# Copying one set of mask rows on VectorE in slot 22 instead of with a DMA

## The chip, the cores and the metric

The kernel runs on one NeuronCore of one Trainium2 chip. The metric is the device time of one execution in microseconds (us), taken as the median of several runs. Five engines run their own instruction streams: TensorE (PE, with its weight loads shown as PEld), VectorE (DVE), ScalarE (ACT), GpSimd (POOL) and SyncE (SP), which here issues DMAs and does nothing else.

## What is computed

Block-sparse attention is followed by a gated feed-forward layer with spatial mixing:

```python
# q, k, v: (batch 4, heads 8, seq 768, dim 64); blocks of 32, so 24 blocks
scores = np.matmul(q, k.transpose(0, 1, 3, 2)) / np.sqrt(64)
mask = near_diagonal | first_or_last_block | sampled_blocks     # per (query block, key block)
attn = softmax(np.where(mask, scores, -1e9))
x = concat_heads(attn @ v)                                       # (4, 768, 512)
h = np.maximum(x @ w_in, 0)                                      # (4, 768, 1024)
u, vv = h[..., :512], h[..., 512:]
vn = (vv - mean(vv)) / np.sqrt(var(vv) + 1e-6)
out = (u * (w_spatial @ vn + b_spatial)) @ w_out
```

## The kernel before, in words

**The mask as matmul rows.** One SBUF tile, `kq`, holds for each of the 8 heads the transposed keys (768 columns, `K_`) and the transposed queries (768 columns, in three thirds of 256 that `qcols(t)` names). Its partitions 0 to 63 are the head dimension. Its partitions 64 to 87 (`MR`) are 24 "block rows": on the key side a one-hot code of the key's block, on the query side the mask value of that query's block against each of the 24 key blocks. A matmul over all 88 partitions so gives score plus mask at once. The block rows are the same for every head and every batch, so they are made once for head 0 and then copied to the other heads. Who copies which piece, and when, differs from piece to piece:

- head 1 gets its rows by VectorE copies (`rows(H1, ...)`) ahead of the loop;
- heads 2 and 3, second query third, by a DMA that SP issues (`rows_dma(1, 4)`);
- heads 2 to 7, third query third, by another DMA that SP issues (`rows_dma(2, H)`); it stands in SP's order behind the last load of `w_in` and in front of the load of `b_col`;
- all other pieces by VectorE copies (`rows`, line 248) in slots that the list `ROWS` names.

**Slots.** The main loop `for s in range(...)` goes through slots. In each slot PE makes one score tile (`qk_unit`, line 446, in slots 0 to 35, where the first batch is done by thirds of the queries; `qk_full`, line 459, after that), ACT takes its exponential, PE makes earlier attention products (`av_unit`, line 492; `av_full`, line 510), then the functions registered with `when(slot, ...)` run, then some steps of the feed-forward layer (`run_queue`, line 584, with the counts of `STEPS`), then the functions in `late`. The order in which this Python code runs is the order of each engine's instructions; nothing is reordered later. The third query third of head 2 is first read by `qk_unit` in slot 27 (unit 9, that is heads 2 and 3).

**What stands in slots 13 to 32 for batch 1 (pairs 4 and 5) and the spatial weights.** SP's order after `rows_dma(2, H)` is: `b_col` (line 364); the loads of pair 4, k, q and v (line 109, slot 13); six loads `ws_f` of the spatial weights (line 550, slots 16 to 18); the DMA transpose `tr_dma` of pair 4 (line 417, slot 20); the loads of pair 5 (slot 22); transposes of the spatial weights (line 560). POOL's order is: the last casts of `w_in` (line 234) and of pair 0's remaining query columns; the casts of pair 4 (line 137, slot 18); `ws_cast` 0, 1 and 2 (line 556, slots 19, 21, 23); the reciprocal deviation `std`, `rstd` of the first two feed-forward rows (lines 623 and 625, slot 23); `ws_cast` 3 (slot 25); the casts of pair 5 (slot 26). VectorE normalises these rows with `rstd` (`vn<-vn,mv,rstd`, line 186), copies the transposed keys and queries of pair 4 into `kq` (`split`, line 218, slots 31 and 32), and empties PSUM banks of the attention product (`xt<-ps_av`, line 218), which PE needs back.

In slot 21 VectorE copies the last queries of pair 0 (`tr_rest(0)`, two copies `kq<-ps_av`). In slot 22 the next VectorE instruction is the ReLU of the feed-forward row v1 (`vn<-ps_moe`, line 186).

Of the kernel before, what the change touches and what calls it, by code (L numbers as in the profile page):

```python
# [26 lines left out]
def kernel(  # L27
# [16 lines left out]
    nc = tc.nc  # L44

    B, H, S, D = q.shape
    BLK = 32
    NB = S // BLK
# [16 lines left out]
    TW = TC * 128  # L65
# [17 lines left out]
    kq = const.tile([KR, H, 2 * S], BF16, name="kq")  # L83
    NVV = 6
    vv = [const.tile([128, 2, NCH, VS], BF16, name=f"vv{s}") for s in range(NVV)]
    MR = slice(D, KR)
    K_, Q_ = slice(0, S), slice(S, 2 * S)

    def qcols(t0, n=1):
        return slice(S + t0 * TW, S + (t0 + n) * TW)  # L90
# [27 lines left out]
    def cast(p, nm, eng, hs=BOTH, cs=ALLC):  # L118
        if nm == "v":
            dst = vv[p % NVV][:, hs, cs, 0:D]  # L120
        else:
            if p not in nat:
                nat[p] = work.tile([128, 2 * NCH, 2, D], BF16, tag="nat", bufs=4, name="nat")
            c0 = 0 if nm == "k" else NCH
            dst = nat[p][:, c0 + cs.start:c0 + cs.stop].rearrange("p c h d -> p h c d")[:, hs]
        src = st[nm, p].rearrange("p h (c d) -> p h c d", d=D)[:, hs, cs]
        if p == 0 and nm != "v":
            dst = nat0_view()[:, hs, (c0 + cs.start) * D:(c0 + cs.stop) * D]
            if cs is not C45:
                dst = dst[:, 0].rearrange("p (i t d) -> p t i d", t=2, d=D)  # L130
                src = src[:, 0].rearrange("p (t i) d -> p t i d", t=2)
            else:
                dst = dst.rearrange("p h (c d) -> p h c d", d=D)
        if eng is nc.scalar:
            nc.scalar.activation(out=dst, in_=src, func=AF.Copy)
        else:
            eng.tensor_copy(out=dst, in_=src)  # L137
# [92 lines left out]
    def w_in_load(u, g):  # L230
        w_load((u, g), moe_w_in[g * 128:(g + 1) * 128, 0 if u else DH:DH if u else DFF])
# [11 lines left out]
    def rows(hs, cs, eng=nc.vector):  # L243
        src = kq[MR, 0:1, cs].to_broadcast([NB, hs.stop - hs.start, cs.stop - cs.start])
        if eng is nc.scalar:
            nc.scalar.activation(out=kq[MR, hs, cs], in_=src, func=AF.Copy)
        else:
            eng.tensor_copy(out=kq[MR, hs, cs], in_=src)  # L248

    def rows_dma(t, h1):  # L250
        nc.sync.dma_start(out=kq[MR, 2:h1, qcols(t)],
                          in_=kq[MR, 0:1, qcols(t)].to_broadcast([NB, h1 - 2, TW]))

    cast(0, "k", nc.scalar, H0, C03)
    cast(0, "q", PL, H0, C03)
    rows(H1, K_)
# [72 lines left out]
    m1()  # L329
    m2()  # L330
    rows(H1, qcols(0, 3))
    rows_dma(1, 4)
    w_in_load(0, 1)
    load(2, "q", cs=C25)
    w_in_load(0, 2)
# [14 lines left out]
    cast(3, "v", PL)  # L350
    w_in_cast(0, 1, PL)
    w_in_load(1, 2)
    rows_dma(2, H)
    cast(2, "q", PL, cs=C25)
    w_in_cast(0, 2, PL)
    w_in_cast(0, 3, PL)
# [376 lines left out]
    def when(slot, *fns):  # L733
        at.setdefault(slot, []).extend(fns)

    def c(f, *a, **kw):
        return lambda: f(*a, **kw)

    ROWS = [(1, 2, 4, qcols(0)), (1, 2, 3, K_), (3, 3, 4, K_), (4, 4, 6, qcols(0)), (6, 4, 6, K_), (7, 6, 8, qcols(0)), (9, 6, 8, K_), (15, 4, 8, qcols(1))]
    when(0, second)  # L740
    when(1, third)
    when(2, lambda: filler(FILL3, psum.tile([128, 512], FP32, tag=moe_tag(), bufs=1, name="wps")))
# [3 lines left out]
    when(10, c(tr_first, 3))  # L746
    for sl, h0, h1, cs in ROWS:
        when(sl, c(rows, slice(h0, h1), cs))
# [146 lines left out]
```

## Time and profile before

| | |
|---|---|
| median of 3 runs | 211.81 us (211.39 to 212.13) |
| the profiled execution | 212.83 us |
| its span, first to last instruction | 209.9 us, so 2.9 us lie around it |
| granted TensorE clock, mean | 0.997 |
| busy: PE, PEld, DVE, ACT, POOL | 200.5, 127.1, 133.7, 167.7, 69.7 us |

Busy times are sums over the span. They do not say where the time is set: that is read from the chain of waits and from the idle gaps of PE, stage by stage. All durations below are of the one profiled execution.

### The profile page before, as it was taken

To read this page: it belongs to the slowest core of one execution; us is meant where nothing else is said; L and a number is where in the kernel's file an instruction comes from. 1 tells how busy PE (TensorE), PEld (TensorE's weight loads), DVE (VectorE), ACT (ScalarE), POOL (GpSimd) and SP (SyncE) were. 2 spreads that over 40 slices of the span, in tenths; PEclk is the share of its full clock that TensorE was granted. 3 is DMA by queue.
4 is the path that set the end of the run, shared out by engine and by line. 5 is a ranking of instruction groups with operands and counts; after the bars stand their busy time and mean duration, and the time that the engine had idled before them with its cause. 6 is when DMAs were issued, how large, how long until landed. Compare 5 with 4: busy or idle time off the path is not lost.

```text
span 209.9 us, 5241 instructions
## 1 busy us (share of the span) xinstructions
PE 200.5 (96%) x2107; PEld 127.1 (61%) x2141; DVE 133.7 (64%) x294; ACT 167.7 (80%) x222; POOL 69.7 (33%) x108
## 2 busy tenths in 40 slices
PE   7898999899999999999999999999999999999992
PEld 6597878666666666665565556665565556544441
DVE  7899675988864545484986464375884443476551
ACT  5898999899989989989998888979999787266021
POOL 6685759675564123033065050131020000012000
PEclk9999999999999999999999999999999999999998
DMA  5999899999999999999955597795101225520275
GB/s 146 343 363 324 279 352 253 272 232 249 275 350 241 257 185 285 242 293 336 209 194 112 131 246 167 202 269 159 37 3 35 52 53 118 196 78 0 50 191 211
DMA packets 64356, 41.93 MB, mean 200 GB/s; under 512 B 45196, under 2 KB 59084, under 8 KB 64332
## 3 DMA queue, kind: packets, MB, share of 16 engines
q1 hardware_dynamic: 63756, 41.01, 75.7%
q10 hardware_dynamic: 576, 0.59, 0.8%
q8 instruction: 16, 0.26, 0.6%
q14 instruction: 8, 0.07, 0.1%
HBM read 24.38 MB, written 6.29 MB: 146 GB/s over the span
## 4 chain that ended last, share of the span: by engine, by line
PE 78%; DVE 6%; DMA 5%; POOL 3%; SPq 2%; issue 2%; ACT 1%; ACTq 0%; DVEq 0%
PE ps_moe L584 29%; PE ps L459 22%; PE ps_av L510 12%; PE ps_t L584 8%; PE ps_sc L584 4%; DMA ws_f<-in_moe_w_spatial_dram 3%; POOL ws_b L556 2%; DVE kq L218 2%; DMA st_q<-in_q_dram 2%; DVE vn L186 2%; SPq L109 2%; PE ps_av L492 1%; PE ps L446 1%; DVE kq L248 1%; PE ps L293 1%
## 5 line engine op out<-in xcount | busy, mean ns | idle before, releaser
L463 ACT ACTIVATE a_all<-ps 128x768 bf16<-128x768 f32 x144 | 113.6, 812 | 14.5 <-PE ps L459 8.2
L459 PE MATMUL ps<-kq 88*128 88x384 bf16 x288 | 70.4, 325 | 0.4
L510 PEld LDWEIGHTS <-a_all 128*128 128x128 bf16 x864 | 45.2, 97 | 20.0
L510 PE MATMUL ps_av<-vv,a_all 128*128 128x65 bf16 x864 | 49.8, 193 | 0.0
L459 PEld LDWEIGHTS <-kq 88*128 88x128 bf16 x288 | 27.7, 98 | 29.6
L584 PE MATMUL ps_moe<-w_in_t,xt 128*128 128x512 bf16 x127 | 38.6, 378 | 0.5
L451 ACT ACTIVATE a_all<-ps 128x1024 bf16<-128x1024 f32 x36 | 34.2, 1026 | 3.0 <-PE ps L446 2.7
L584 PE MATMUL ps_moe<-vn,w_spt 128*128 128x512 bf16 x99 | 30.2, 378 | 0.4
L137 POOL CAST nat<-st_k 128x768 bf16<-128x768 f32 (+2 forms) x17 | 13.2, 781 | 39.6 <-DMA st_k<-in_k_dram 38.0
L446 PE MATMUL ps<-kq 88*128 88x256 bf16 (+1 forms) x140 | 21.6, 275 | 2.0 <-ACT a_all L451 0.9
L656 DVE SCALAR_TENSOR_TENSOR un<-ps_moe,b_col,un 128x512 bf16<-128x512 f32 x18 | 13.4, 746 | 13.6 <-PE ps_moe L584 11.3
L623 POOL TENSOR_SCALAR std<-mv 128x3 f32<-128x3 f32 (+1 forms) x9 | 2.2, 240 | 58.2 <-DVE mv L620 41.1
L474 DVE RECIPROCAL rc<-ps_av 128x6 f32<-128x6 f32 (+1 forms) x36 | 6.6, 183 | 21.5 <-PE ps_av L510 20.0
L584 PEld LDWEIGHTS <-xt 128*128 128x128 bf16 x192 | 15.5, 98 | 7.6 <-DVE xt L218 0.2
L584 PE MATMUL ps_moe<-w_out_t,gt 128*128 128x512 bf16 x66 | 19.7, 378 | 0.2
L475 DVE TENSOR_TENSOR xn<-ps_av,rc 128x384 bf16<-128x384 f32 (+1 forms) x36 | 18.5, 513 | 1.2
L137 POOL CAST nat<-st_q 128x768 bf16<-128x768 f32 (+2 forms) x21 | 14.8, 706 | 8.5 <-DMA st_q<-in_q_dram 8.2
L619 DVE BATCH_NORM_STATS2 stats<-vn 128x6 f32<-128x512 bf16 x24 | 16.4, 684 | 1.3 <-ACT vn L614 0.9
L137 POOL CAST vv<-st_v 128x768 bf16<-128x768 f32 x16 | 13.8, 863 | 9.4 <-DMA st_v<-in_v_dram 9.0
L186 DVE TENSOR_SCALAR vn<-vn,mv,rstd 128x512 bf16<-128x512 bf16 x24 | 14.0, 615 | 4.4 <-POOL rstd L625 4.4
L218 DVE COPY kq<-tt 64x1536 bf16<-64x1536 bf16 x24 | 14.8, 618 | 2.9 <-DMA tt<-nat 2.6
L446 PEld LDWEIGHTS <-kq 88*128 88x128 bf16 x140 | 12.5, 97 | 5.8 <-DVE kq L218 1.9
(81 smaller groups left out, 202.5 us busy)
## 6 DMA issues: line engine op xcount, KB each, us to landing
st_v<-in_v_dram SPq DMA_DIRECT2D x16, 384.0 KB, 6.1
st_k<-in_k_dram SPq DMA_DIRECT2D x15, 384.0 KB, 4.5
out_dram<-osb SPq DMA_DIRECT2D x22, 256.0 KB, 3.1
st_q<-in_q_dram SPq DMA_DIRECT2D x12, 384.0 KB, 5.6
ws_f<-in_moe_w_spatial_dram SPq DMA_DIRECT2D x6, 384.0 KB, 7.6
w_f<-in_moe_w_in_dram SPq DMA_DIRECT2D x8, 256.0 KB, 5.5
w_f<-in_moe_w_out_dram SPq DMA_DIRECT2D x4, 256.0 KB, 4.0
st_q<-in_q_dram SPq DMA_DIRECT2D x6, 128.0 KB, 5.8
```

Of the source, the lines that this page charges most:

```text
L137: eng.tensor_copy(out=dst, in_=src)
L186: nc.vector.tensor_scalar(out=out, in0=in0, scalar1=s1, scalar2=s2, op0=o0, **kw)
L218: nc.vector.tensor_copy(out=o, in_=i)
L446: nc.tensor.matmul(out=ps[:, at:at + n * TW], lhsT=kq[:, h, ci * 128:(ci + 1) * 128], rhs=kq[:, h, qcols(t0, n)], start=True, stop=True)
L451: nc.scalar.activation(out=out, in_=ps, func=AF.Exp, scale=0.125)
L459: nc.tensor.matmul(out=ps[:, hf * 512:hf * 512 + HALF], lhsT=kq[:, j % H, ci * 128:(ci + 1) * 128], rhs=kq[:, j % H, S + hf * HALF:S + (hf ...
L463: nc.scalar.activation(out=a_ref["h", j][:, ci, :].rearrange("p (b c) -> p b c", b=2), in_=ps.rearrange("p (b c) -> p b c", b=2)[:, :, 0:H ...
L475: nc.vector.tensor_tensor(out=out, in0=ps[:, :, 0:D], in1=rc[:, 0:n].to_broadcast([128, n, D]), op=ALU.mult)
L510: nc.tensor.matmul(out=av_ref[j][:, qc, 0:VA], lhsT=a_ref["h", j][:, ci, qc * 128:(qc + 1) * 128], rhs=vv[p % NVV][:, h, ci, 0:VA], start= ...
L584: nc.tensor.matmul(out=ref["ps"][:, 0:w], lhsT=lhs(i), rhs=rhs(i), start=(i == 0), stop=(i == n - 1))
L619: nc.vector.bn_stats(out=stats, in_=self.vn[:, tcc, :])
L656: nc.vector.scalar_tensor_tensor(out=self.un[:, tcc, :], in0=ps, scalar=b_col[:, tcc:tcc + 1], in1=self.un[:, tcc, :], op0=ALU.add, op1=AL ...
```

## The change

The DMA for heads 2 to 7 of the third query third goes out of SP's order. In its place the list `ROWS` gets one more entry, so VectorE makes the same copy (24 partitions, 6 heads of 256 columns) in slot 22. The helper `rows_dma` goes away; its other use is written out and stays what it was.

```diff
-    def rows_dma(t, h1):
-        nc.sync.dma_start(out=kq[MR, 2:h1, qcols(t)],
-                          in_=kq[MR, 0:1, qcols(t)].to_broadcast([NB, h1 - 2, TW]))
...
     rows(H1, qcols(0, 3))
-    rows_dma(1, 4)
+    nc.sync.dma_start(out=kq[MR, 2:4, qcols(1)],
+                      in_=kq[MR, 0:1, qcols(1)].to_broadcast([NB, 2, TW]))
...
     w_in_load(1, 2)
-    rows_dma(2, H)
     cast(2, "q", PL, cs=C25)
...
-    ROWS = [(1, 2, 4, qcols(0)), ... (9, 6, 8, K_), (15, 4, 8, qcols(1))]
+    ROWS = [(1, 2, 4, qcols(0)), ... (9, 6, 8, K_), (15, 4, 8, qcols(1)), (22, 2, 8, qcols(2))]
     when(0, second)
     when(1, third)
...
     for sl, h0, h1, cs in ROWS:
         when(sl, c(rows, slice(h0, h1), cs))
```

More of the change, by code (lines that the diff above doesn't have):

```diff
@@ L737, in c @@
         return lambda: f(*a, **kw)
-    ROWS = [(1, 2, 4, qcols(0)), (1, 2, 3, K_), (3, 3, 4, K_), (4, 4, 6, qcols(0)), (6, 4, 6, K_), (7, 6, 8, qcols(0)), (9, 6, 8, K_), (15, 4, 8, qcols(1))]
+    ROWS = [(1, 2, 4, qcols(0)), (1, 2, 3, K_), (3, 3, 4, K_), (4, 4, 6, qcols(0)), (6, 4, 6, K_), (7, 6, 8, qcols(0)), (9, 6, 8, K_), (15, 4, 8, qcols(1)), (22, 2, 8, qcols(2))]
     when(0, second)
```

## The prediction

> **What bounds the kernel now.** I read the busy time by stretches first, then the chain of waits, then the order of time of SP, POOL, DVE and PE around the change. The stretches (columns: length; busy us of PE, PEld, DVE, ACT, POOL; clock; DMA share; GB/s), and the sum of five longer ones from 42 to 206 us:
>
> ```profile
> 20.00:24.00 4.00, 3.95 (x64) 3.36 (x62) 2.84 (x9) 3.88 (x5) 3.35 (x6) 1.00 0.90 284
> 24.00:28.00 4.00, 3.92 (x57) 3.22 (x57) 2.75 (x8) 3.71 (x5) 2.37 (x5) 1.00 0.88 292
> 28.00:32.00 4.00, 3.94 (x57) 3.23 (x57) 3.44 (x9) 3.91 (x5) 2.58 (x3) 1.00 1.00 352
> 36.00:40.00 4.00, 3.43 (x39) 2.54 (x38) 3.24 (x5) 3.85 (x5) 3.09 (x3) 1.00 1.08 336
> ```
>
> ```profile
> sum 164.00, PE 162.34 PEld 95.90 DVE 100.21 ACT 130.81 POOL 40.26; mean PE 32.47 PEld 19.18 DVE 20.04 ACT 26.16 POOL 8.05
> ```
>
> The reader is to see that PE is the bound nearly everywhere: the last row is the sum of 42 to 206 us, over which PE is busy 162.34 of 164 us. A time won or lost before 42 us is therefore carried to the end almost unchanged, and nothing can be won after it. From 20 us on only one stretch has a hole, 36 to 40 us, with 4.00 - 3.43 = 0.57 us. The chain of waits says where the hole comes from:
>
> ```profile
> 20.76 0.24 SPq L251
> 21.00 0.05 issue
> 21.05 0.51 SPq L364
> 21.56 0.06 issue
> 21.62 0.42 SPq L109
> 22.04 0.04 issue
> 22.09 1.56 SPq L109
> 23.64 0.04 issue
> 23.69 0.47 SPq L109
> 24.16 0.04 issue
> 24.20 6.75 DMA ws_f<-in_moe_w_spatial_dram
> 30.95 0.05 issue
> 31.00 4.60 POOL ws_b L556 x3
> ...
> 36.00 0.74 POOL rstd L625
> 36.76 1.65 DVE vn L186
> ```
>
> From 20.76 on it runs through SP's instructions one behind the other, and L251 is the DMA that the change takes away. The first `ws_f` lands at 30.95, POOL casts three pieces, computes `rstd`, and VectorE can then normalise. What this costs PE stands in the order of time of DVE and then of PE (a bracket is idle time before the instruction, and what ended it):
>
> ```profile
> 36.76 1.65 DVE L186 TENSOR_SCALAR vn<-vn,mv,rstd 128x512 bf16<-128x512 bf16 x1 [0.99 <-POOL rstd L625]
> 38.81 1.05 DVE L186 TENSOR_SCALAR vn<-vn,mv,rstd 128x512 bf16<-128x512 bf16 x1
> 39.78 0.27 DVE L218 COPY xt<-ps_av 128x256 bf16<-128x256 bf16 x1
> ```
>
> ```profile
> 40.10 0.65 PE L492 MATMUL ps_av<-vv,a_all 128*128 128x65 bf16 x16 [0.68 <-DVE xt L218]
> ```
>
> DVE idles 0.99 us until `rstd`, works through `vn`, the `kq` copy and `vn` again, and only then empties the PSUM bank that PE needs: PE idles 0.68 us. So an earlier `rstd` is worth its advance, one for one, up to 0.68 us, and nothing beyond.
>
> **What the change removes.** SP and the loads that follow:
>
> ```profile
> 17.74 2.34 SPq L228 DMA_DIRECT2D w_f<-in_moe_w_in_dram  x4
> 20.18 0.82 SPq L251 DMA_DIRECT2D kq<-kq  x1
> ```
>
> and the size of the removed DMA, from the list of DMA issues:
>
> ```profile
> kq<-kq SPq DMA_DIRECT2D x1, 72.0 KB
> ```
>
> The four `w_f` issues end at 20.08. The removed DMA starts at 20.18 and `b_col` at 21.05. Without it `b_col` can start at 20.18, so everything behind it on SP (`b_col`, the three loads of pair 4, the six `ws_f`, the transpose of pair 4, the loads of pair 5) may be issued 21.05 - 20.18 = 0.87 us earlier. Nothing else on SP changes its order, and what stands ahead of 20.18 is untouched, so no load is issued later: a loss on SP is excluded.
>
> How much of the 0.87 us reaches `ws_f` depends on whether issue or transfer rate holds the loads. If only the rate does, the gain is the 72 KB that are no longer moved: 73,700 bytes at 284 GB/s (first row above) = 0.26 us. If issue does, it is 0.87 us. The rows speak for something between: 284 and 292 GB/s in 20 to 28 us stand against 352 GB/s in 28 to 32, so some (68 + 60) x 4 us = 510 KB more would have gone through, or 510/352 = 1.45 us at full rate. The transfers were not always full and can take earlier work. Against it, the q load at 22.09 took SP 1.56 us where its neighbours took 0.42 and 0.47, so something ahead of SP was full for about 1.1 us, and that may simply wait longer. I take the middle, (0.26 + 0.87)/2 = 0.57 us.
>
> POOL must be able to use it:
>
> ```profile
> 26.37 0.83 POOL L137 CAST nat<-st_k 128x768 bf16<-128x768 f32 x1
> 27.92 0.83 POOL L137 CAST nat<-st_q 128x768 bf16<-128x768 f32 x1 [0.72 <-DMA st_q<-in_q_dram]
> 30.06 0.83 POOL L137 CAST vv<-st_v 128x768 bf16<-128x768 f32 x1 [1.31 <-DMA st_v<-in_v_dram]
> ```
>
> It waits 0.72 and 1.31 us for loads of pair 4 and then goes on into `ws_b` with no gap that matters. Both the cast of v (ends 30.89) and the first `ws_f` (lands 30.95) stand just before 31.00, and both are behind the removed DMA. With 2.03 us of waiting in front of it POOL is not the limit. So `rstd` comes 0.57 us earlier, and PE gains 0.57 of its 0.68 us.
>
> **What the change adds.** One DVE copy of 24 partitions x 1536 elements. The same line has two of that size; the rows of DVE and PE around its place follow:
>
> ```profile
> L248 DVE COPY kq<-kq 24x1536 bf16<-24x1536 bf16 x2 | 1.1, 573 | 0.0
> ```
>
> ```profile
> 26.83 0.58 DVE L218 COPY kq<-ps_av 64x256 bf16<-64x256 bf16 x2
> 28.25 0.69 DVE L186 TENSOR_SCALAR vn<-ps_moe 128x512 bf16<-128x512 f32 x1 [0.84 <-PE ps_moe L584]
> ```
>
> ```profile
> 32.34 0.60 PE L446 MATMUL ps<-kq 88*128 88x256 bf16 x4
> ```
>
> In slot 22 it stands between the two DVE rows shown after it: DVE is free at 27.41 and idles 0.84 us until PE has the row v1 ready at 28.25. The copy, 0.573 us, ends at 27.98. Its cost is 0, and its cover is that gap; 0.27 us are left. Its source, the mask of head 0, is written ahead of the loop, and nothing has read its target, so it adds no wait on DVE. Queued behind it are the ReLU of v1 and what follows on DVE. Its first reader is the QK of slot 27, which by counting the L446 groups back from slot 35, the last, is the PE row of 32.34, 4.4 us after it. PE, which waited for a DMA there, now waits for an older DVE instruction, at no cost. The upper end is a copy that POOL holds up (a DVE row, then rows of POOL):
>
> ```profile
> 14.30 0.89 DVE L248 COPY kq<-kq 24x512 bf16<-24x512 bf16 x1
> ```
>
> ```profile
> 14.22 0.83 POOL L137 CAST vv<-st_v 128x768 bf16<-128x768 f32 x1 [0.23 <-DMA st_v<-in_v_dram]
> 36.69 1.57 POOL L556 CAST ws_b<-ws_f 128x768 bf16<-128x768 f32 x1
> 38.89 0.83 POOL L137 CAST nat<-st_k 128x768 bf16<-128x768 f32 x1 [0.63 <-PE ps L446]
> ```
>
> A third of the size took 0.89 us beside a POOL cast that started 0.08 us ahead of it, and ended with the cast (15.05) plus 0.14; in the same way the `vn` of 36.76 took 1.65 us beside the cast of 36.69. A DVE copy between SBUF tiles can so lose a whole POOL cast. If the cast of pair 4's q (27.92 now) came to stand just ahead of the copy, it would end at 27.41 + 0.83 + 0.57 = 28.81, and DVE would be 28.81 - 28.25 = 0.56 us late for v1. PE shows no wait on DVE from 28 to 36 us, so I cost this at 0 too, with 0.56 us as the upper end. It adds work, so below nothing is excluded.
>
> The Trainium skill, page "SBUF — State Buffer", section "Who interferes with whom", says that DVE in a 2-port mode and GpSimd take a shared port pair for a whole instruction and the other fully blocks; this speaks against putting the copy on DVE. The rows of 14.30 and 36.76 agree with it. By it the copy could also hold POOL for its 0.57 us, and the sum would still be that above, since POOL waits 0.72 us for st_q there.
>
> **Sum.** -0.57 (earlier `rstd`) + 0 (copy) = -0.57 us, 0.27%. The profiled execution, 212.83 us (span 209.9 and 2.9 around it), would become 212.26; it stands 1.02 us over the median of the runs, 211.81, to which I apply the same difference: **211.3 us**. A measurement of this kernel can tell about 0.3%, or 0.64 us, from no change.
>
> **Rivals.**
>
> *A, the forecast:* gain between 0.35 and 0.75 us (0.68 is PE's hole, the rest is the spread of reading it), 211.1 to 211.5. For it: the chain of waits runs through the removed instruction. Against: the 1.56 us of the q load.
>
> *B, the transfers hold the loads anyway:* SP's earlier issue only queues longer, and the gain is the bytes, 0.26 us, or less: 211.5 to 211.8, middle 211.6. For it: 352 GB/s in 28 to 32 us, where `ws_f` is under way. It also holds the case that the change does nothing at all. The Trainium skill, page "DMA: Bandwidth & Descriptors", section "Issuing engines are not separate DMA queues", calls the sequencer's issue time usually small against the DMA itself, which would make this the case. The trace disagrees in part, with 0.82 us of issue here.
>
> *C, slower: one more POOL cast in DVE's way.* The place is DVE's stretch from 36.76 to 39.86 that ends PE's hole. POOL is free there from 38.26 (36.69 + 1.57) to 38.89, when the cast of pair 5's k begins, and DVE gets its `kq` copy in at 38.34. If the loads of pair 5 come forward by more than these 0.63 us against POOL's `rstd`, that cast begins before the copy and the copy waits 0.83 us. The second `vn` can then lose again to the cast of q. PE's hole grows by up to 0.83 us, and PE carries it to the end: 211.81 + 0.83 = 212.6. Less, down to no loss, if the second `vn` then goes free. For it: loads 0.87 us earlier are what the change allows, and if `ws_f` gains least the order can flip. Against it: `rstd` and the loads of pair 5 hang on the same SP order and should move together.
>
> **How the numbers follow.** A 0.47, B 0.22, C 0.31. C gets that much since the rows of 14.30, 36.76 and 38.81 show three such meetings of DVE and POOL already, and a shift of the loads can make others. Of A, 0.30 lies over 0.64 us of gain, if most of the 0.87 us arrives and PE's hole closes, and 0.17 under it. B lies within 0.3%. Of C, 0.26 lies over a loss of 0.64 us and 0.05 under it. So faster by over 0.3%: 0.30; within: 0.17 + 0.22 + 0.05 = 0.44; slower: 0.26. The range goes from 210.9 (hole closed, 211.1, and 0.2 us for the spread of the runs) to 212.6 (C at its price). It leaves out the part of C in which two casts get in the way. A's own range is 211.1 to 211.5.
>
> **What would show it.** Right: `b_col` issued near 20.2, the first `ws_f` near 23.3 and landed near 30.4; `rstd` near 35.4; PE's idle time before the L492 group near 40 us down to about 0.1; the copy of 24x1536 between the two `kq<-ps_av` copies and the ReLU of v1, 0.57 us long. Wrong: `ws_f` landing at 30.7 or later (B); DVE's copy from `tt` or the second `vn` over 1.1 us long near 38 us and PE's hole larger (C); the new copy near 0.9 us or more and PE idle between 28 and 36 us (the upper end of its cost). The forecast fails whole if PE idles after 42 us where it did not before.

## The result and the profile after

| | before | after |
|---|---|---|
| median of the runs compared (22 of each) | 211.46 us (210.41 to 213.29) | 210.83 us (209.88 to 211.97) |
| ratio after / before | | 0.996, 95% interval 0.9941 to 0.9979 |
| the profiled execution | 212.83 us | 211.1 us |
| its span | 209.9 us | 209.3 us |

The change made the kernel faster by 0.4%: 0.63 us by the medians, 0.85 us by the ratio, whose interval reaches from 0.44 to 1.25 us. The predicted time was 211.3 us (-0.57 us, -0.27%) with a range from 210.9. The median after the change so lies just under that range. Later comparisons, below, make the gain smaller: three of the same two kernels give 0.9970 together. Executions in a slower state, with a granted clock of 0.992 (two of t4's twelve and four of w4's, below), are left out of every ratio.

The page of after, its busy line and the head of its chain of waits:

```profile
span 209.3 us, 5241 instructions
...
PE 202.5 (97%) x2107; PEld 128.6 (61%) x2141; DVE 132.5 (63%) x295; ACT 167.7 (80%) x222; POOL 69.4 (33%) x108
...
PE 90%; DVE 4%; ACT 2%; issue 2%; ACTq 0%
```

DMA, POOL and SP's queue no longer stand in the chain: the stretch that the prediction followed through SP, `ws_f`, POOL and `rstd` has left it. The stretches of after (columns: length; busy us of PE, PEld, DVE, ACT, POOL; clock; DMA share; GB/s) and the sum from 42 to 206 us:

```profile
20.00:24.00 4.00, 3.95 (x68) 3.54 (x67) 3.59 (x11) 3.88 (x5) 2.10 (x4) 1.00 1.07 359
24.00:28.00 4.00, 3.92 (x59) 3.17 (x58) 2.64 (x8) 4.00 (x5) 3.24 (x7) 1.00 1.01 361
28.00:32.00 4.00, 3.94 (x51) 3.10 (x51) 3.65 (x9) 3.62 (x5) 3.90 (x4) 1.00 1.01 398
36.00:40.00 4.00, 3.96 (x50) 3.14 (x50) 3.82 (x10) 3.85 (x5) 2.76 (x4) 1.00 1.13 353
```

```profile
sum 164.00, PE 162.27 PEld 95.97 DVE 99.30 ACT 130.79 POOL 39.26; mean PE 32.45 PEld 19.19 DVE 19.86 ACT 26.16 POOL 7.85
```

Transfers run at 359 GB/s from 20 us on where they had 284, PE's hole between 36 and 40 us is gone (3.96 busy instead of 3.43), and after 42 us PE is as busy as before (162.27 against 162.34). Read alone, these rows say that the forecast came true. SP and POOL in after:

```profile
20.22 0.42 SPq L360 DMA_DIRECT2D b_col<-in_moe_b_spatial_dram  x1
...
23.63 3.57 SPq L546 DMA_DIRECT2D ws_f<-in_moe_w_spatial_dram  x6
```

```profile
27.88 0.83 POOL L137 CAST nat<-st_q 128x768 bf16<-128x768 f32 x1
28.81 0.99 POOL L137 CAST vv<-st_v 128x768 bf16<-128x768 f32 x1
29.79 3.08 POOL L552 CAST ws_b<-ws_f 128x768 bf16<-128x768 f32 x2
33.43 1.55 POOL L552 CAST ws_b<-ws_f 128x768 bf16<-128x768 f32 x1 [0.56 <-DMA ws_f<-in_moe_w_spatial_dram]
...
35.38 0.72 POOL L621 TENSOR_TENSOR rstd<-std,mhalf 128x2 f32<-128x2 f32 x1
```

`b_col` is issued at 20.22 (21.05 before), the first `ws_f` at 23.63 (24.20), and `rstd` starts at 35.38 (36.00). DVE in after:

```profile
27.73 0.58 DVE L218 COPY kq<-ps_av 64x256 bf16<-64x256 bf16 x2
28.34 0.78 DVE L248 COPY kq<-kq 24x1536 bf16<-24x1536 bf16 x1
29.15 0.69 DVE L186 TENSOR_SCALAR vn<-ps_moe 128x512 bf16<-128x512 f32 x1
...
36.58 1.20 DVE L186 TENSOR_SCALAR vn<-vn,mv,rstd 128x512 bf16<-128x512 bf16 x1
37.71 0.54 DVE L218 COPY kq<-tt 64x1536 bf16<-64x1536 bf16 x1
38.18 0.40 DVE L186 TENSOR_SCALAR vn<-vn,mv,rstd 128x512 bf16<-128x512 bf16 x1
38.50 0.28 DVE L218 COPY xt<-ps_av 128x256 bf16<-128x256 bf16 x1
```

The copy stands where it was put; it took 0.78 us and not 0.573, and POOL's cast of q runs from 27.88 to 28.71 beside it. `vn` no longer waits for `rstd`, and PE's group `ps_av` at 40.16 has no idle time before it.

**But that is not where the 0.6 us of the two spans came from.** The same PE instructions in the two profiles: the QK of slot 27 began at 32.34 before, and the first `qk_full` at 41.81. In after these are

```profile
33.23 0.60 PE L442 MATMUL ps<-kq 88*128 88x256 bf16 x4
...
41.87 0.49 PE L455 MATMUL ps<-kq 88*128 88x384 bf16 x2
```

So after was 0.89 us *behind* in slot 27, and at 42 us, with the hole gone, still 0.06 behind. At the issue of the last output it was only 0.07 ahead (ACTq rows below). The rest lies in the closing rows of the program, which do no work of the kernel. Their groups show durations as min/median/max in ns, then the first and the last start. Before:

```profile
206.40 0.35 ACTq L685 DMA_DIRECT2D out_dram<-osb  x1
```

```profile
L890 SPq EVENT_SEMAPHORE  x7: 17/28/1592, 206.5 to 209.8; - x7
...
L890 SPq DRAIN  x3: 7/7/137, 209.0 to 209.4; - x3
```

And after:

```profile
206.33 0.35 ACTq L681 DMA_DIRECT2D out_dram<-osb  x1
```

```profile
L886 SPq EVENT_SEMAPHORE  x7: 17/28/1539, 206.4 to 209.3; - x7
...
L886 SPq DRAIN  x3: 7/8/13, 208.6 to 209.1; - x3
```

From the issue of the last output to the end of the span there are 209.9 - 206.40 = 3.5 us before and 209.3 - 206.33 = 3.0 us after (to 0.1 us). SP's first closing DRAIN starts at 209.0 in the one and 208.6 in the other, and the longest of its three takes 137 ns in the one and 13 ns in the other. The semaphore waits ahead of it are much alike (the longest 1592 and 1539 ns). This led to a second theory: the gain comes from a closing part that is shorter because SP's program is one DMA shorter, and not from the earlier loads.

### The profile page after: what moved, and what is told of

It is laid out like the page before. It is cut to its first block, busy times and chain, and to the rows that moved or that the text cites. A ratio compares the mean times of both kernels' runs of the same rounds, so it can differ in the third digit from the quotient of the medians.

```text
span 209.3 us, 5241 instructions
## 1 busy us (share of the span) xinstructions
PE 202.5 (97%) x2107; PEld 128.6 (61%) x2141; DVE 132.5 (63%) x295; ACT 167.7 (80%) x222; POOL 69.4 (33%) x108
## 4 chain that ended last, share of the span: by engine, by line
PE 90%; DVE 4%; ACT 2%; issue 2%; ACTq 0%
PE ps_moe L580 31%; PE ps L455 22%; PE ps_av L506 12%; PE ps_t L580 8%; PE ps L442 6%; PE ps_sc L580 4%; PE ps_av L488 3%; DVE kq L218 2%; PE wps L180 2%; ACT a_all L447 1%; DVE kq L248 1%; PE ps L289 1%; PE ps_av L289 1%; ACT osb L221 0%; ACT a_all L459 0%
## 5 line engine op out<-in xcount | busy, mean ns | idle before, releaser
L455 PEld LDWEIGHTS <-kq 88*128 88x128 bf16 x288 | 27.7, 97 | 29.7
L442 PE MATMUL ps<-kq 88*128 88x256 bf16 (+1 forms) x140 | 23.2, 290 | 0.6 <-ACT a_all L447 0.2
L442 PEld LDWEIGHTS <-kq 88*128 88x128 bf16 x140 | 13.0, 101 | 4.8 <-DVE kq L218 0.7
L580 PEld LDWEIGHTS <-w_spt 128*128 128x128 bf16 x144 | 11.6, 98 | 5.6
```

The lines of the kernel that those rows point to most:

```text
L442: nc.tensor.matmul(out=ps[:, at:at + n * TW], lhsT=kq[:, h, ci * 128:(ci + 1) * 128], rhs=kq[:, h, qcols(t0, n)], start=True, stop=True)
L455: nc.tensor.matmul(out=ps[:, hf * 512:hf * 512 + HALF], lhsT=kq[:, j % H, ci * 128:(ci + 1) * 128], rhs=kq[:, j % H, S + hf * HALF:S + (hf ...
L580: nc.tensor.matmul(out=ref["ps"][:, 0:w], lhsT=lhs(i), rhs=rhs(i), start=(i == 0), stop=(i == n - 1))
```

## The experiments

Theory L (the prediction's): loads issued earlier make `rstd` earlier and PE's hole smaller. Theory E: the loads have slack in most executions, and the gain is the closing part. The expectations were written as the theories grew: "theory S" in the first four is L's first link (SP's issue time ahead of the loads is what costs) and "rival T" says that the DMA's bytes are; "H" is the gain from PE's hole alone. All ratios are to the kernel before in the same session, with 95% intervals; "closing" is the time from the issue of the last output (the ACTq row) to the end of the span, to 0.1 us.

| kernel | ratio | interval | closing, us | `rstd` starts, us |
|---|---|---|---|---|
| before, again (u1) | 0.999 | 0.997 to 1.0011 | 3.5 | 34.65 |
| after, again (u2) | 0.9997 | 0.9971 to 1.0023 | 3.0 | 33.86 |
| after, a third time (w1) | 0.9963 | 0.9939 to 0.9987 | 2.9 | 34.73 |
| e1, DMA of one head | 1.0015 | 0.9987 to 1.0042 | 3.5 | 33.72 |
| e2, DMA earlier | 1.0029 | 1.0004 to 1.0054 | 3.5 | 34.76 |
| e3, before with b_col later | 0.9995 | 0.9973 to 1.0017 | 3.5 | 34.12 |
| e4, DMA and copy | 0.9986 | 0.9963 to 1.001 | 3.5 | 35.00 |
| t1, after with one DMA more, late | 1.001 | 0.9988 to 1.0031 | 3.5 | 33.86 |
| w2, the same again | 0.9982 | 0.9961 to 1.0004 | 3.5 | 34.54 |
| u3, after with two DMAs more, late | 1.0002 | 0.9982 to 1.0022 | 3.6 | 33.42 |
| t2, before with one output on ACT | 0.9988 | 0.9967 to 1.0009 | 3.0 | 35.99 |
| u4, before with two outputs on ACT | 0.9997 | 0.9977 to 1.0017 | 3.2 | 34.21 |
| t3, after with b_col later | 0.998 | 0.9964 to 0.9996 | 3.0 | 34.16 |
| t4, two copies | 1.0017 | 0.9988 to 1.0045 | 3.0 | 34.86 |
| w3, before with one DMA more, early | 1.0017 | 0.9996 to 1.0038 | 3.6 | 36.28 |
| w4, before with three DMAs more, early | 1.0033 | 1.0008 to 1.0058 | 3.4 | 37.06 |

**Does issue or do bytes hold the loads? e1** keeps the DMA for head 2 alone (12 KB in place of 72) and lets VectorE copy the other five heads.

```diff
-    rows_dma(2, H)
+    rows_dma(2, 3)
...
-    ROWS = [(1, 2, 4, qcols(0)), ... (15, 4, 8, qcols(1))]
+    ROWS = [(1, 2, 4, qcols(0)), ... (15, 4, 8, qcols(1)), (22, 3, 8, qcols(2))]
```

> The DMA stays in its place in SP's order but fills head 2 only (12 KB in place of 72 KB); VectorE copies heads 3 to 7 in slot 22. So SP issues as many DMAs as before, and five sixths of the bytes are gone. Theory S (SP's issue slot ahead of the loads is what cost): as before, ratio 1.000 give or take 0.002, b_col issued near 21.0. Rival T (the bytes and packets of the DMA are what cost): as the changed kernel, near 0.996, since five sixths of the cause are gone. In between, by SP's issue being shorter for fewer packets, if both have a part.

```profile
19.60 0.79 SPq L251 DMA_DIRECT2D kq<-kq  x1
20.44 0.50 SPq L364 DMA_DIRECT2D b_col<-in_moe_b_spatial_dram  x1
```

A sixth of the bytes took 0.79 us of SP's time, against 0.82 for all of them: SP's time does not go with the bytes. The ratio, 1.0015, shows no gain from the 60 KB less. It does not choose between L and E: SP issues as many DMAs as before, so both expect no gain.

**The DMA at another place. e2** issues it behind `rows_dma(1, 4)`.

```diff
     rows_dma(1, 4)
+    rows_dma(2, H)
...
     w_in_load(1, 2)
-    rows_dma(2, H)
```

> The same DMA of 72 KB, issued some 9 us earlier, right behind the DMA for heads 2 and 3, where SP still has waits ahead of it (the two last w_in loads wait for POOL). No copy on VectorE. Theory S: the loads of pair 4 move forward as in the changed kernel, ratio near 0.996, PE's hole near 40 us gone. Rival T: the bytes still pass, only earlier, in a stretch where the transfers are full (361 to 366 GB/s from 8 to 17 us), so up to half of the gain or none: 0.998 to 1.000. Against S it could also delay the loads ahead of 20 us, by 0.2 us for the bytes or 0.8 us for the issue; then slower than before and PE idle between 10 and 20 us.

`b_col` went out at 19.94, earlier than in after, and `rstd` started at 34.76; yet the kernel was slower, 1.0029. By theory L it should have gained. But it also moves other things (the `w_f` and q loads behind it now come later), and its profile has the slow start of TensorE that the last section describes, so it does not decide against L by itself.

**The loads earlier with the DMA in place. e3** takes b_col's DMA out of the way instead.

```diff
-    nc.sync.dma_start(out=b_col, in_=moe_b_spatial.rearrange("(p c) -> p c", c=NCH))
...
+    when(32, lambda: nc.sync.dma_start(out=b_col, in_=moe_b_spatial.rearrange("(p c) -> p c", c=NCH)))
```

> The kernel before, with the 3 KB load of b_col moved from just behind the DMA to slot 32, behind the loads and transposes there. It frees 0.57 us of SP (21.05 to 21.62) ahead of the loads of pair 4 and hardly any bytes, 128 packets of 24 bytes. Theory S: ratio near 0.9975 (0.5 us of the hole closed), rstd 0.4 to 0.6 us earlier against PE. Rival T: 1.000.

0.9995: no gain that can be told from loads that may go some 0.5 us earlier, though the interval, from 0.9973, still holds the 0.9975 expected by theory S. **t3** is the same edit on after.

> The changed kernel, with the load of b_col moved to slot 32: another 0.5 us of SP is freed ahead of the loads of pair 4, on top of the 0.87 us of the change. If the hole near 40 us still takes part of the executions after the change, 0.1 to 0.3 us more: 0.995. If it is closed, 0.996 as the changed kernel. The end is as in the changed kernel, 2.9 us, if the count of DMAs or the length of SP's program sets it.

Its 0.998 is within after's own figures (0.996 to 0.9997): nothing more is gained that can be told.

**The copy alone. e4** keeps the DMA and makes the copy too.

```diff
-    ROWS = [(1, 2, 4, qcols(0)), ... (15, 4, 8, qcols(1))]
+    ROWS = [(1, 2, 4, qcols(0)), ... (15, 4, 8, qcols(1)), (22, 2, 8, qcols(2))]
```

> Both: the DMA stays as before, and VectorE copies the same rows once more in slot 22. It shows the cost of the copy alone. Theory (the copy lies in VectorE's gap in slot 22): ratio 1.000 give or take 0.002. Rival (the copy costs, by its own length or by POOL holding it up): up to 1.0027, and VectorE's ReLU of v1 late.

0.9986, no cost that can be told: the copy lies in VectorE's gap, as predicted. In its trace the copy takes 0.55 us, and DVE then still idles 0.26 us until PE has the row v1 ready. **t4** makes the copy twice in after.

> The changed kernel with the copy made twice, one behind the other, in slot 22: 2 x 0.57 = 1.15 us of VectorE in a gap of 0.84 us, so the ReLU of v1 comes 0.3 us late, 0.5 us if POOL holds a copy. If VectorE's lateness there reaches PE, 0.3 to 0.5 us slower than the changed kernel, 0.9975 to 0.9985; if it has slack there as the waits of PE say, 0.996.

DVE, and what PE waited for, in t4:

```profile
28.34 3.04 DVE L248 COPY kq<-kq 24x1536 bf16<-24x1536 bf16 x2
31.41 0.69 DVE L186 TENSOR_SCALAR vn<-ps_moe 128x512 bf16<-128x512 f32 x1
```

```profile
PE ps_av L488 <- DVE xt L218: 1.4, 1, 1.4
```

Two copies took 3.04 us where two alone would take 2 x 0.573 = 1.15: POOL cast q, v and the first `ws_b` from 27.32 on with hardly a pause, and the copies stood beside these casts. The ReLU of v1 came at 31.41, and PE stood still for 1.4 us. The ratio is 1.0017 where after has 0.9970. So the cover of the copy is real but narrow: one copy fits, two do not. The Trainium skill, page "SBUF — State Buffer", section "Who interferes with whom", has DVE in a 2-port mode and GpSimd lock each other out for a whole instruction; by that rule whichever issues first goes through. The rows agree: beside a cast that had begun, the one copy took 0.76 to 1.08 us (after, t1, t3, u3, w1); with no cast ahead of it, it took 0.55 us (u2, w2), and in w2 POOL paid (copy at 28.37, POOL's cast of v from 28.37 on 1.24 us instead of 0.83).

**Is it the closing part? t1** lengthens SP's program again without touching the early loads: the last load of `w_out`, in slot 44, is issued in two halves.

```diff
-        w_load(("o", g), moe_w_out[g * 128:(g + 1) * 128, :])
+        if g < 3:
+            w_load(("o", g), moe_w_out[g * 128:(g + 1) * 128, :])
+            return
+        wst["o", g] = work.tile([128, DM], FP32, tag="osb", bufs=6, name="w_f")
+        for cs in (slice(0, DM // 2), slice(DM // 2, DM)):
+            nc.sync.dma_start(out=wst["o", g][:, cs], in_=moe_w_out[g * 128:(g + 1) * 128, cs])
```

> The changed kernel, with the last load of w_out (slot 44, a stretch in which no chain of waits runs through it) cut into two DMAs of half the size. So SP again issues as many DMAs as before the change, and the stretch from 20 to 40 us is that of the changed kernel. Theory E (of the gain, 0.5 us is made at the end: from the last output DMA's issue to the span's end the changed kernel took 2.9 us in its profile and every kernel with one DMA more 3.4 us, since the count of DMAs or SP's code decides the closing waits): the end takes 3.4 us again, and the ratio to before rises from 0.996 to 0.9985, the 0.3 us of earlier loads being what is left. Rival H (all of the gain is PE's hole near 40 us): the ratio stays at 0.996.

1.001: the gain is gone, and the closing part is back at 3.5 us. The second DMA itself costs nothing that shows ahead of the end: in the profiles of t1, u3 and w2 the last output is issued at 206.09, 205.76 and 206.34 us, in those of after, u2 and w1 at 206.33, 206.46 and 205.97. **t2** goes the other way: the kernel before, with one output in the middle issued by ACT, so that SP's program is one DMA shorter and the early DMA stays.

```diff
-                    (nc.scalar if i or (self.last and tcc == 0) else nc.sync).dma_start(
+                    (nc.scalar if i or (self.last and tcc == 0) or (self.b == 2 and tcc == 2) else nc.sync).dma_start(
```

> The kernel before, with one output DMA of the third batch issued by ACT in place of SP: SP has one DMA less in its program, as after the change, the count of all DMAs stays, and the stretch around the hole is untouched. If SP's shorter program sets the short end, the end takes 2.9 us and the ratio is 0.9976. If the count of all DMAs sets it, the end takes 3.4 us and the ratio is 1.000. Rival H: 1.000.

Closing 3.0 us, as in after; the issue of the last output, and SP's closing group:

```profile
206.60 0.34 ACTq L685 DMA_DIRECT2D out_dram<-osb  x1
```

```profile
L890 SPq EVENT_SEMAPHORE  x7: 17/28/1616, 206.6 to 209.5; - x7
```

The ratio, 0.9988, holds both 0.9977 (half a us) and 1 in its interval, so t2 shows the shorter closing part in the trace but not in the time. Then came both kernels again, and one DMA more in either direction.

> The kernel before, unchanged, for a second profile. In its first profile PE idled 0.68 us near 40 us; three other kernels that keep the DMA in its place (12 KB, b_col later, DMA and copy) showed no such hole. If the hole is in most executions, it is here again. If it depends on when the loads happen to land in an execution, it is likely absent, and the span is 208.9 to 209.0 us with TensorE at full clock from 3.8 to 5.3 us on, some 0.7 us more where the full clock comes at 9.4 to 10.1 us. From the last output DMA's issue to the span's end: 3.4 us again.

> The changed kernel, unchanged, for a second profile and a second comparison. Theory E plus H (0.5 us at the end, the rest a hole that only some executions have): ratio 0.996 to 0.9975, the end takes 2.95 us again, no hole near 40 us. If the clock comes early in its profile (3.8 to 5.3 us) the span is near 208.5 us, if late near 209.3.

> The changed kernel with the last two loads of w_out cut into two DMAs each, so SP issues one DMA more than before the change. If the length of SP's program decides the end as in the profiles so far (2.95 us with one DMA less, 3.4 to 3.5 us with the old number), it is one more look at which lengths are long: 3.4 if only the changed length is short, another value if it goes by steps. With a long end the ratio is 0.998 to 1.000, of which the rest is the hole; with a short one 0.996.

> The kernel before with two output DMAs of the third batch issued by ACT in place of SP; the DMA and the stretch around the hole stay. SP's program is two DMAs shorter, that of ACT two longer. A short end (2.95 us) would say that every shorter program of SP does it, and the ratio is 0.9975 if theory E holds; a long one that the one length of the changed kernel is meant, and the ratio is 1.000.

u1, the kernel before against itself, gives 0.999, which is what a comparison can be off by. u2 gives 0.9997 for after, where the first comparison gave 0.996: a single comparison did not settle a gain of this size. u3 (SP's program one DMA longer than before's) shows 3.6 us and no gain. u4 (two shorter) shows 3.2 us and not less than t2's 3.0: the closing part is not simply longer with each DMA. Its ratio is 0.9997. Weighted by their intervals, t2 and u4 give 0.9993 (0.9978 to 1.0007), where a closing part shorter by 0.5 and 0.3 us would give about 0.998: the interval just holds that, and it holds no gain as well. So a shorter closing part by itself was not shown to pay. What it costs that ACT issues these outputs was not measured apart. For these reasons four more kernels were run.

> The changed kernel, unchanged. If its gain is the shorter closing part alone: 0.49 us, ratio 0.9977, and from the last output's issue to the end of the span 2.95 us. If the earlier loads bring their 0.57 us on top: 0.995. If the first comparison was a lucky draw and there is no gain: 1.000.

> The changed kernel with one load of w_out cut into two DMAs, late in the kernel, so that SP's program is as long as before. Closing part alone: the gain is gone, ratio 1.000, and 3.45 us from the last output's issue to the end. Earlier loads: the gain stays, 0.997.

w1 is faster (0.9963) with 2.9 us at the end; w2, equal to t1, stands at 0.9982 with 3.5. Weighted by their intervals, the three comparisons of after give 0.9970 (0.9957 to 0.9983), and the three of after with the end restored (t1, u3, w2) 0.9998 (0.9986 to 1.0010). The difference, 0.28% or 0.6 us with 0.4 either way, agrees with what the traces show at the end, about 0.5 us. What is left for the earlier loads is at most 0.14%, 0.3 us; the 0.57 us of the forecast are outside. The mean spans of these runs say the same, each to about 0.1 us: 209.6 us for the kernel before, 209.0 for after, 209.5 for t1, u3 and w2. The 209.45 of t2 and u4 does not fit theory E alone, which wants some 209.2 there.

**What slack do the loads have? w3 and w4** put one and three small DMAs (12 KB each, of rows that nobody reads) behind the one in question, so that everything behind them goes out later. The edit of w3 is shown; in w4 both ones are threes.

```diff
+    spare = const.tile([KR, 1, TW], BF16, name="spare")
...
     rows_dma(2, H)
+    for i in range(1):
+        nc.sync.dma_start(out=spare[MR, i:i + 1],
+                          in_=kq[MR, 0:1, qcols(2)].to_broadcast([NB, 1, TW]))
```

> The kernel before with one more small DMA (12 KB, of rows nobody reads) behind the one that the change removes: loads behind it are issued some 0.8 us later, and SP's program is one DMA longer. If the loads have no slack (the prediction's view), PE's hole near 40 us grows by up to 0.8 us: ratio 1.003 to 1.004. If they have slack: 1.000. The closing part may also grow, by up to some tenths of a us, which the rows of the end tell apart.

> The same with three more small DMAs: loads some 2.4 us later. No slack: 1.011, with PE idle by some 2 us before its L492 group near 40 us. Slack of about 1 us: 1.005 to 1.007. Slack of over 2.4 us: 1.000 but for the closing part.

Here theory L's chain is seen at work. POOL, DVE and PE of w3:

```profile
36.28 0.72 POOL L629 TENSOR_TENSOR rstd<-std,mhalf 128x2 f32<-128x2 f32 x1
```

```profile
37.04 1.66 DVE L187 TENSOR_SCALAR vn<-vn,mv,rstd 128x512 bf16<-128x512 bf16 x1 [1.08 <-POOL rstd L629]
38.62 0.54 DVE L219 COPY kq<-tt 64x1536 bf16<-64x1536 bf16 x1
39.09 0.91 DVE L187 TENSOR_SCALAR vn<-vn,mv,rstd 128x512 bf16<-128x512 bf16 x1
39.92 0.27 DVE L219 COPY xt<-ps_av 128x256 bf16<-128x256 bf16 x1
```

```profile
40.24 0.65 PE L496 MATMUL ps_av<-vv,a_all 128*128 128x65 bf16 x16 [0.63 <-DVE xt L219]
```

This is the profile of before over again: a late `rstd`, both `vn` long, the bank late, PE idle 0.63 us, and 0.39 us once more until 42.83. In w4 `b_col` goes out at 23.85 and `rstd` starts at 37.06, but the hole does not stand near 40 us: the second `vn` took 0.40 us, PE itself came later, and a stall of 0.59 us behind DVE's `vn` ends at 51.77 instead. The times rise with the delay, +0.36 us for one DMA (0.82 us of SP's time; interval -0.1 to +0.8) and +0.70 us for three (3.10 us of SP's time; interval 0.2 to 1.2), with a closing part that differs from before's by 0.1 us at most. So later loads cost some quarter of their delay (w4), and earlier ones bring nothing that could be measured. That fits loads that have slack in most executions of the kernel before and little of it in some.

## Why the prediction was right and wrong

**SP's part was right.** `b_col` moved forward by 0.83 us and the first `ws_f` by 0.57 (23.3 was forecast, 0.9 us), and POOL began on it at 29.79 without waiting, where a landing near 30.4 was forecast. e1 showed that issue and not bytes costs SP the time. That the 0.57 us came out to the digit is luck: they were the middle between two bounds, and taken for want of a row that decides. **The advance of `rstd` agrees, but is not shown to be more than chance.** It was 0.62 us in the two first profiles. Over seven profiles each, kernels with the DMA in its place (before, u1, e1, e3, e4, t2, u4) have it at 34.81 us on average, and kernels without (after, u2, w1, t1, u3, w2, t3) at 34.28: 0.53 us earlier, against 0.57 forecast. Single profiles scatter around these means by 0.7 to 0.9 us, so the difference could as well be zero or 1 us.

**The step that failed** is "So an earlier `rstd` is worth its advance, one for one, up to 0.68 us". It held for the execution that was profiled, and it was priced as if it held for every one. Across the seven profiles with the DMA `rstd` starts anywhere from 33.72 to 36.00 us, a spread four times the advance; the profile of before drew the latest. In u1, the same kernel, POOL's `rstd` and DVE read

```profile
34.65 0.72 POOL L625 TENSOR_TENSOR rstd<-std,mhalf 128x2 f32<-128x2 f32 x1
```

```profile
36.13 0.42 DVE L475 TENSOR_TENSOR xn<-ps_av,rc 128x256 bf16<-128x256 f32 x1
36.47 0.60 DVE L186 TENSOR_SCALAR vn<-vn,mv,rstd 128x512 bf16<-128x512 bf16 x1
37.12 0.55 DVE L218 COPY kq<-tt 64x1536 bf16<-64x1536 bf16 x1
37.60 0.40 DVE L186 TENSOR_SCALAR vn<-vn,mv,rstd 128x512 bf16<-128x512 bf16 x1
```

`rstd` is done at 35.37, 1.1 us before DVE comes to `vn` from work of its own, and PE has no hole. Of the seven, only the two with the latest `rstd` have PE wait for this chain at all: before (36.00) and t2 (35.99). In t2

```profile
36.75 1.64 DVE L186 TENSOR_SCALAR vn<-vn,mv,rstd 128x512 bf16<-128x512 bf16 x1 [0.82 <-POOL rstd L625]
...
38.79 0.40 DVE L186 TENSOR_SCALAR vn<-vn,mv,rstd 128x512 bf16<-128x512 bf16 x1
```

no cast of POOL met the second `vn` (0.40 us; 1.05 in before), and PE had no hole near 40 us. But the `rstd` of the next two rows was late in its turn, at 47.75, and PE stood still for 0.77 us, until 50.87, behind the `vn` that hang on it:

```profile
PE ps_moe L584 <- DVE vn L186: 0.8, 1, 0.8
```

So the mechanism is real, and the size is what failed: 0.68 and 0.77 us in two profiles of seven and nothing in the other five make about 0.2 us on average (an estimate from few profiles, of kernels that differ a little) in place of the 0.57 us of the sum. The comparisons leave at most 0.3.

**The term that was missing** is the closing part, 0.5 us in the traces. The prediction said that after 42 us "nothing can be won": true for PE in the one profile that it read (t2 lost 0.77 us behind 42 us), and the rows behind the last output were not looked at. The page's span ends with closing rows of all engines, SP's among them, and SP is where the change takes one DMA away. In time this term is shown from one side: put back, it took the gain away (t1, u3, w2); made alone, it did not bring one that could be told (t2, u4).

**The copy's cost of 0 was right**, its length was not: 0.55 to 1.08 us instead of 0.573, by POOL's cast of q or of v beside it. The upper end that was given, 0.56 us for PE, did not come; t4 shows what it takes. **Rival B** (bytes only, or nothing) had the right size for the loads but the wrong reason: the loads do come earlier, and in most executions are not needed earlier. **Rival C** (POOL's casts in the way near 38 us) did not come in after: its second `vn` took 0.40 us. Such meetings do happen with and without the change (0.94 and 0.91 us in w2 and t3, 0.91 in w3).

That the total, 0.4% in the first comparison and 0.30% in three, lies near the 0.27% forecast is in the main luck: of the 0.57 us at most 0.3 are there, and the rest goes with some 0.5 us at the end that were not in the sum.

**Open:** why SP's closing DRAIN comes later and takes longer when its program has one DMA more. The waits that the traces name for SP's closing rows add up to the same in before and after, 1.9 us for the output DMAs and 0.6 us for PE and SP. In u4 one DRAIN is long as well (130 ns, against 137 in before and 13 in after), so what counts may be where in SP's program the closing rows stand; that is not shown. Why t2 and u4 gain so little is open too, and whether the change has a cost of its own at the start (last section). That the earlier loads bring exactly nothing is not shown either, only that it is under 0.3 us. And the kernels' spread from one execution to the next, some 2 us, is larger than all effects here.

## What to carry to other kernels

A hole in one profile is worth its length only if other executions have it too: before pricing it, look how early its last releaser would be needed, and take a second profile of the same kernel where that can be had. Read the rows behind the last output as well, since a DMA fewer in an engine's program can shorten them. A gain under half a per cent needs several comparisons, and a version that undoes just the suspected part (here a DMA issued in two halves, late) says more than one more run of the change.

## What the runs showed of the hardware

**The closing part.** It took 2.9 to 3.0 us in every profile with one DMA less in SP's program than before's (after, u2, w1, t2, t3, t4), 3.5 us with as many (before, u1, e1 to e4, t1, w2), 3.6 with one more (u3, w3), 3.4 with three more (w4) and 3.2 with two less (u4).

**An SBUF copy by DMA cost SP about 0.8 us at both sizes tried:** 0.82 us for 72 KB and 0.79 for 12 KB in e1, where the load of `b_col` takes 0.42 to 0.51 us.

**TensorE's early matmuls have two speeds.** At 6 us the group of four QK matmuls takes 1.06 us in after

```profile
6.31 1.06 PE L442 MATMUL ps<-kq 88*128 88x256 bf16 x4
...
8.55 0.63 PE L180 MATMUL wps<-warm 128*128 128x128 bf16 x4
```

and 0.60 us in before:

```profile
5.83 0.60 PE L446 MATMUL ps<-kq 88*128 88x256 bf16 x4 [0.23 <-DVE kq L218]
...
7.20 0.39 PE L180 MATMUL wps<-warm 128*128 128x128 bf16 x4
```

In after the matmuls are still slow at 9 us; that fits its being 0.89 us behind in slot 27. The profiles of u2, t1, t3, t4, e2, w2 and w4 have the slow start too, those of w1, u1, u3, u4, e1, e3, e4, t2 and w3 the fast one, so the same program (after and w1) has both. The clock column of the profile does not tell them apart: it reads 1.00 from 4 to 12 us in before and in after. Of the eight profiles without the early DMA six have the slow start, and none of the seven with the DMA in its place has it. Whether the change makes that start more frequent was not tested; if it does, part of what the earlier loads bring is lost there, and the bound of 0.3 us above is what is left after that loss. The Trainium skill, page "TensorE: Matmul & The Clock Gate", section "What's actually happening", has a clock that is halved until a free-running window of 3.4 us was busy, and a transition that varies by 0.5 us either way; the rows agree with the two speeds, but the slow start lasted at least 4 us longer in after (still slow at 9 us) than in before (fast at 4.93 us).
